# Hash attention and a gated feed-forward on one core: the second pair's hash bits, the bound's judgement, the flag read and the last additions

## The chip, the core and the metric

The kernel runs on one core of a Trainium2 chip. PE is TensorE (its weight loads, PEld, overlap its products), DVE is VectorE, ACT is ScalarE, POOL is GpSimd and SP is SyncE, which here only issues transfers. The metric is the device time in microseconds (us) of one execution. The kernel before the change has a median of 904.65 us over three runs (904.62 to 905.37).

## The reference

Two blocks follow each other. The first is attention over hash buckets: 4 batches of 8 heads, 768 positions, head dimension 64. Six sign bits of a projection give each query and key a bucket, and a key counts only for queries of its bucket. The second is a feed-forward layer with a gate of its own, over 3072 tokens, 512 wide and 2048 inside.

```python
q_bits = (np.einsum('bhsd,dk->bhsk', q, proj) > 0)      # and k_bits
mask = q_bucket[:, :, :, None] == k_bucket[:, :, None, :]
scores = np.where(mask, scale * q @ k.transpose(0, 1, 3, 2), -1e9)
attn = softmax(scores)                                  # exp(s - max) / (sum + 1e-9)
x = (attn @ v).transpose(0, 2, 1, 3).reshape(3072, 512)
h = x @ w_in
sp = np.maximum(h, 0.0) + np.log1p(np.exp(-np.abs(h)))
out = (h * erf(sp)) @ w_out
```

## The kernel before

**Attention.** Two heads form a pair, one on partitions 0 to 63 and one on 64 to 127; there are 16 pairs. A pair has four *scores* (two halves of the queries by two groups of keys), each in three chunks of 128 keys. For a chunk PE adds two products in PSUM: one over the hash bits in bf16, in which a key of another bucket gets a large negative term, and one over q and k in fp32. ACT takes the exponential, PE *weighs* the values with it, and DVE sums the exponentials over the key blocks. For the sum over partitions, the *divisor*, PE multiplies by a tile of ones. No maximum is subtracted; the kernel measures squared norms of q and k instead (`measure`, ACT) and judges later whether the bound on the scores holds (`judge`, L1743 to L1771). If it does not, the branch behind `flag` (L1776, L1777) computes everything again in a general way.

**Hash bits.** For pairs 0 and 1 they come by `hash_bits` (L377): four products with 64 output columns, into both banks of a PSUM tile. ACT takes the sign, DVE scales and doubles it in place, in `both[0]` or `both[1]`. For pairs from 2 on, `bits_of` (L845) makes four products with 32 output columns into one bank, `sign_of` (L854) and `weigh_bits` (L864) work on one [128, 384] tile, `leave_bits` (L874) writes it to DRAM and `place_bits` (L883) reads it back, as two transfers of POOL, into the rows that the scores use. The unused rows of `both[n]` must be zero; `clean` (L903) clears them on POOL after pair n's scores.

**Feed-forward.** Both products follow a scheme with seven products for eight blocks. A block p of 48 has the first products P1 to P7, which `read` (ACT) and `complete` (DVE, L1270) assemble into h, the gate (sigmoids on ACT at L1278 and L1282, multiplications on DVE at L1288), and the second products M1 to M7 (`project`, L1361). Eight blocks make a tile of 512 tokens; at its end `combine` (L1396) adds the seven banks into the output, in steps 0 to 8. The last two steps, 7 and 8, each take one half of the bank of M3. In the last tile (`t == NTILE - 1`) their results are sent from ACT's queue.

**Order.** Inside `tc.manual_schedule()` the instructions stand on each engine in the order in which they are emitted. `arrange` makes that order: a greedy planner with a cost, a rank, predecessors (`after`) and a delay to other engines (`late`) for every step. It runs once for attention and once for the feed-forward part. In attention PE's steps form one chain: the four scores of a pair, its four weighings, the bits of the pair after next and the divisor of the pair before; the bits of pair 1 stand between pair 0's scores and weighings. `start_pair` issues a pair's six transfers on SP. The weights are fetched as 32 pieces, two on SP and the rest on POOL, and converted on ACT and DVE alongside attention. The judgement is one step, `("check", 0)`, booked as 0.3 us of PE; it also carries five groups of DVE's instructions. Waits between engines are derived from the tiles that instructions read and write, in the order of emission.

Of the kernel before, what the change touches and what calls it, by code (L numbers as in the profile page):

```python
# [54 lines left out]
F32 = mybir.dt.float32  # L55
# [141 lines left out]
def kernel(  # L197
# [11 lines left out]
    nc = tc.nc  # L209
    B, H, S, D = v.shape  # L210
# [138 lines left out]

    def fetch(i, load, quick=False):  # L350
        d = dict(
            q=load.tile([P, S], F32, name="q", tag="q"),
            k=load.tile([P, S], F32, name="k", tag="k"),
            v=load.tile([P, NC, P], F32, name="v", tag="v"),
        )
        b, j = divmod(i, JP)
        parts = ((0, "q"), (0, "k"), (1, "k"), (1, "q")) if quick else ((None, "q"), (None, "k"))
        for half, what in parts:
            cols = slice(0, S) if half is None else slice(half * HS, half * HS + HS)
            queue = nc.scalar if quick and what == "k" and half == 0 else nc.sync  # L360
            for ab in range(2):
                queue.dma_start(
                    out=d[what][ab * D : ab * D + D, cols],
                    in_=qkT[2 * i + ab, "qk".index(what) * D : "qk".index(what) * D + D, cols],
                )
        for ab in range(2):
            nc.sync.dma_start(
                out=d["v"][:, :, ab * D : ab * D + D],
                in_=v[b, 2 * j + ab].rearrange("(c p) d -> p c d", p=P),
            )  # L370
        return d

# [47 lines left out]
    def attention():  # L420
        NS = NPAIR * 4
        with (
# [17 lines left out]
            e_even = ep.tile([P, NE, 2, HS + 1], F32, name="e_even")  # L440
            nc.vector.memset(e_even[:, :, :, HS : HS + 1], 1.0)
            e_odd = area[:, 0 : NE * S].rearrange("p (n a c) -> p n a c", n=NE, a=2)
            e_last = {}
# [226 lines left out]
            def divisor(i):  # L670


                d = pairs[i]
                if i == NPAIR - 1:
                    z = bank("z_ps")[:, 0:HS]
                else:
                    if i == NPAIR - 2:
                        room = pairs[i - 1]["z_room"]
                    else:
                        room = pairs[i + 3]["bits"] if i + 3 < NPAIR else big("z_ps")  # L680
                        d["z_room"] = room
                    z = room[:, 0 if i == NPAIR - 2 else 1, 0:HS]
                d["z_ps"] = z
                for half in range(2):
                    for n in range(4):
                        ab, part = divmod(n, 2)
                        nc.tensor.matmul(  # L687
                            out=z[n * QR : (n + 1) * QR, half * HS // 2 : (half + 1) * HS // 2],
                            lhsT=ones[:, 0:QR],
                            rhs=d["sum"][:, half, ab, part * HS // 2 : (part + 1) * HS // 2],  # L690
                            start=True,
                            stop=True,
                        )

# [27 lines left out]
            def spread(i):  # L722

                d = pairs[i]
                zd = d["zd"] = dram.tile([2, 4, HS // 2], F32, name="zd", tag="zd")
                d["zc"] = small.tile([P, 2 * S // P], F32, name="zc", tag="zc")
                nc.sync.dma_start(
                    out=zd.rearrange("h n c -> n h c"),
                    in_=d["z"][0 : 3 * QR + 1 : QR, 0:HS].rearrange("n (h c) -> n h c", h=2),
                )  # L730

            def gather(i):
# [3 lines left out]
                    in_=d.pop("zd")  # L736
                    .rearrange("h n c -> (h n c)")
                    .rearrange("(p c) -> p c", c=2 * S // P),
# [62 lines left out]
            def start_pair(i):  # L801
                pairs[i] = fetch(i, load)

# [30 lines left out]
            def bits_of(i):  # L834


                if i == 1:
                    hash_bits(pairs[i], big)
                    return
                d = pairs[i]  # L840
# [48 lines left out]

            def place_first():  # L890

                cols = slice(0, S)
                sign_bits(pairs[1], lambda what: both[1][:, "qk".index(what[0]), :], cols)

            def weigh_first(ab):
                spread_bits(pairs[1], slice(0, S), ab)

            def double_first():
                double_bits(pairs[1], slice(0, S))

            def clean(n):
# [6 lines left out]
            for i in range(NPAIR):  # L908
                order += [("score", 4 * i + k) for k in range(4)]
                if i == 0:  # L910
                    order.append(("bits", 1))
                order += [("weigh", 4 * i + k) for k in range(4)]
# [7 lines left out]
            for what, n in order:  # L920
                free = slots[-3] if len(slots) >= 3 else ()
                if what == "score":
                    i = n // 4
                    after = (("double_first",) if i == 1 else ("place_bits", i),)
                    for c in range(GC):
# [3 lines left out]
                elif what == "bits":  # L929
                    pe(bits_of, (n,), 0.80 if n > 1 else 1.44, (("start_pair", n),) + free)  # L930
                    slots.append((("sign_of", n),) if n > 1 else (("place_first",),))
                elif what == "divisor":
# [53 lines left out]
            for i in range(NPAIR):  # L986
                n = 4 * i
                if i:
# [3 lines left out]
                        "SP",  # L992
                        3.6,
                        (0, n - 6),
                        (("weigh", n - 9), ("bits_of", i - 1))
                        + tuple(("measure", i - 3, m, half) for m in range(2) for half in range(2)),
                        late=3.5,
                    )
                    if i == 1:
                        op(place_first, (), "ACT", 0.9, (0, n - 2, 9), (("bits_of", i),))  # L1000
                        for ab in (1, 0):
                            op(weigh_first, (ab,), "DVE", 0.43, (0, n - 2, 1), (("place_first",),))
                        op(double_first, (), "DVE", 0.35, (0, n - 2, 2), (("weigh_first", 0), ("weigh_first", 1)))
                    else:
                        op(sign_of, (i,), "ACT", 0.6, (0, n - 6, 9), (("bits_of", i), ("leave_bits", i - 1)))
                        op(weigh_bits, (i,), "DVE", 0.33, (0, n - 6, 1), (("sign_of", i),))
                        op(leave_bits, (i,), "POOL", 0.7, (0, n - 6, 2), (("weigh_bits", i),), late=4.0, far=True)
                        op(
                            place_bits,
                            (i,),  # L1010
                            "POOL",
                            1.2,
                            (0, n - 6, 3),
                            (("leave_bits", i), ("score", n - 5, 2), ("clean", i - 2)),
                            late=3.6,
                        )
                for m in range(2):
# [25 lines left out]
                op(send, (i,), "SP", 0.35, (0, n, 4), (("normalise", i),), late=2.2)  # L1043
            for n in range(2):
                op(clean, (n,), "POOL", 1.4, (0, 4 * n), (("score", 4 * n + 3, 2),), late=0.3)
            for n in range(len(pieces)):
# [154 lines left out]
    def feed_forward(check, late):  # L1201
        again = late is None
        with (
# [503 lines left out]
            if late:  # L1707
# [15 lines left out]
                for each in ops:  # L1723
                    if each.name in (("P5", 2), ("P6", 2), ("P7", 2), ("P3", 2)):
                        each.after += (("late", 6),)
                op(("check", 0), "PE", 0.3, (0, 1, 9), check, (), after=(("P3", 0), ("late", 0)), late=1.5)
                for each in ops:
                    if each.name == ("P2", FILL - 1):
                        each.after += (("check", 0),)
            else:  # L1730
                load_x(0)
                for k in range(4):
                    presum_x(0, k)
            for each in arrange(ops, dict(h=8, e=4, w=4, wt=2), PATIENCE):
                each.emit()

    flag = const.tile([1, 1], I32, name="flag")
    norms = const.tile([1, 2, 2, NPAIR], F32, name="norms")
    top = const.tile([1, 1], F32, name="top")

    def judge():

        ps = bank("bound")[:, 0 : 4 * NPAIR]  # L1743
        for ab in range(2):
# [6 lines left out]
                stop=True,  # L1751
            )
        for ab in range(2):
            nc.vector.tensor_reduce(  # L1754
# [3 lines left out]
                op=ALU.max,  # L1758
            )
        both = norms[:, :, 0, :]  # L1760
        nc.vector.tensor_tensor(out=both, in0=both, in1=norms[:, :, 1, :], op=ALU.mult)
# [9 lines left out]
        nc.vector.tensor_scalar(out=flag, in0=top, scalar1=1.0, scalar2=None, op0=ALU.add)  # L1771

    with tc.manual_schedule():
        late = attention()
        feed_forward(judge, late)
    again = nc.values_load(flag[0:1, 0:1], min_val=0, max_val=1)  # L1776
    with tc.If(again > 0):  # L1777
        general()
        feed_forward(None, None)
# [53 lines left out]
```

## Time and profile before

| what | value |
| --- | --- |
| median of three runs | 904.65 us (904.62 to 905.37) |
| the profiled execution, its own time | 904.72 us |
| its span | 902.9 us |
| granted TensorE clock, mean | 0.998 |
| PE busy | 894.3 us (99%), 5016 products |
| DVE / ACT / POOL busy | 668.5 / 563.3 / 57.9 us |
| attention, PE's first score to its last weighing | 6.1 to about 313.5 us |

A row of a group or of a timeline shows the start, the busy time, the engine, the line of the kernel, the operation, what it writes and reads, and in brackets the idle time just before it with what ended it. An engine's name with a q is its sequencer, which reads instructions ahead of the engine. "x8" is a number of instructions. A transfer's line shows the time its issue took; the time to landing is another view.

### The profile page before, as it was taken

What the parts mean: (1) busy time and instruction counts of PE and PEld (TensorE: products, weight loads), DVE (VectorE), ACT (ScalarE), POOL (GpSimd) and SP (SyncE); (2) the same over time, 40 slices, a digit from 0 to 9 for tenths busy, and PEclk for the clock granted to TensorE, in tenths of its full rate; (3) what the DMA queues carried; (4) which work ended last, traced back from release to release, by engine and by line L of the source; (5) the groups of instructions that cost most, each with busy time, mean ns of one, the idle gap of its engine ahead of it and who ended that gap; (6) DMA issues with size and microseconds to landing.
All of it is one profiled execution on the core that took longest, in us unless ns stands there. A gap on an engine that the chain in (4) does not pass through costs nothing.

```text
span 902.9 us, 12780 instructions
## 1 busy us (share of the span) xinstructions
PE 894.3 (99%) x5016; PEld 670.9 (74%) x5016; DVE 668.5 (74%) x837; ACT 563.3 (62%) x808; POOL 57.9 (6%) x95
## 2 busy tenths in 40 slices
PE   9999999999999999999999999999999999999997
PEld 5455554455544588888888888888888888888886
DVE  5999999999999879995666556666776666655652
ACT  6788888788886668855645455545655555545520
POOL 1211211111110000000000001000100010000000
PEclk9999999999999999999999999999999999999999
DMA  9547655667551322202231013211421122111211
GB/s 228 149 128 183 200 166 142 196 173 195 154 157 60 101 89 65 82 36 70 59 106 58 14 49 103 82 36 47 105 83 36 36 74 78 35 36 57 63 68 50
DMA packets 65156, 86.82 MB, mean 96 GB/s; under 512 B 34364, under 2 KB 47772, under 8 KB 65088
## 3 DMA queue, kind: packets, MB, share of 16 engines
q1 hardware_dynamic: 56528, 63.81, 24.8%
q0 software_dynamic: 8112, 21.66, 8.6%
q8 instruction: 41, 0.67, 0.3%
q10 hardware_dynamic: 448, 0.46, 0.2%
q14 instruction: 27, 0.22, 0.1%
HBM read 64.67 MB, written 17.30 MB: 91 GB/s over the span
## 4 chain that ended last, share of the span: by engine, by line
PE 99%; DVE 0%; issue 0%; ACT 0%; DVEq 0%
PE M L1361 32%; PE X L1248 29%; PE st L557 17%; PE av L642 14%; PE M L1248 3%; PE bits L845 1%; PE bits L687 1%; PE warm L807 0%; PE bits L377 0%; PE z_ps L687 0%; DVE e L1288 0%; DVE h L1270 0%; ACT both L390 0%; DVE u L1396 0%; DVE norms L1754 0%
## 5 line engine op out<-in xcount | busy, mean ns | idle before, releaser
L1288 DVE SCALAR_TENSOR_TENSOR e<-w,e 128x1024 f32<-128x1024 f32 x144 | 173.7, 1220 | 8.4 <-ACT w L1282 3.9
L1248 PE MATMUL X<-area,w_in_sb 128*128 128x256 f32 x680 | 160.6, 379 | 0.0
L1282 ACT ACTIVATE w<-h,cq 128x1024 f32<-128x1024 f32 x144 | 155.6, 1136 | 0.1
L557 PE MATMUL st<-q,k 64*128 64x384 f32 x768 | 155.1, 482 | 0.0
L1270 DVE TENSOR_TENSOR h<-X,h 128x512 f32<-128x512 f32 x65 | 44.8, 689 | 144.4 <-PE X L1248 144.4
L1248 PEld LDWEIGHTS X<-area,w_in_sb 128*128 128x128 f32 x680 | 129.2, 190 | 17.6
L1361 PE MATMUL M<-w_out_sb,h 128*128 128x256 f32 x576 | 141.1, 379 | 0.0
L1248 PE MATMUL X<-area 128*128 128x256 f32 x520 | 122.8, 379 | 0.0
L1361 PEld LDWEIGHTS M<-w_out_sb,h 128*128 128x128 f32 x576 | 109.4, 190 | 14.9
L1266 ACT COPY h<-X 128x512 f32<-128x512 f32 x85 | 49.3, 580 | 111.4 <-PE X L1248 111.3
L1248 PEld LDWEIGHTS X<-area 128*128 128x128 f32 x520 | 98.8, 190 | 13.4
L1278 ACT ACTIVATE e<-h,cq 128x1024 f32<-128x1024 f32 x48 | 55.1, 1148 | 85.9 <-DVE h L1270 85.8
L1361 PE MATMUL M<-wt,S 128*128 128x256 f32 x384 | 95.1, 379 | 0.0
L557 PEld LDWEIGHTS st<-q,k 64*128 64x128 f32 x768 | 68.8, 187 | 29.7 <-issue 27.2
L630 DVE TENSOR_TENSOR area<-area 128x1536 f32<-128x1536 f32 (+1 forms) x46 | 79.2, 1723 | 7.5 <-ACT area L584 6.3
L1361 PEld LDWEIGHTS M<-wt,S 128*128 128x128 f32 x384 | 73.0, 190 | 9.9
L584 ACT ACTIVATE e_even<-st 128x768 f32<-128x768 f32 x96 | 70.6, 822 | 0.4 <-PE st L557 0.3
L584 ACT ACTIVATE area<-st 128x768 f32<-128x768 f32 x90 | 68.0, 817 | 0.0
L642 PE MATMUL av<-e_even,v 128*64 128x385 f32 x384 | 65.6, 490 | 0.0
L557 PE MATMUL st<-both 64*128 64x384 bf16 x384 | 63.5, 323 | 0.3 <-ACT both L390 0.3
L1303 DVE TENSOR_TENSOR h<-h,e 128x1024 f32<-128x1024 f32 x48 | 57.9, 1220 | 4.6 <-ACT e L1299 4.6
L642 PE MATMUL av<-area,v 128*64 128x384 f32 x360 | 60.6, 486 | 0.0
(129 smaller groups left out, 976.8 us busy)
## 6 DMA issues: line engine op xcount, KB each, us to landing
wt<-wt SPq DMA_DIRECT2D x24, 768.0 KB, 4.2
raw<-in_w_out_dram POOLq DMA_DIRECT2D x16, 512.0 KB, 4.2
raw<-in_w_in_dram POOLq DMA_DIRECT2D x14, 512.0 KB, 4.6
v<-in_v_dram SPq DMA_DIRECT2D x32, 192.0 KB, 4.6
q<-in_qkT_dram SPq DMA_DIRECT2D x30, 192.0 KB, 4.2
k<-in_qkT_dram SPq DMA_DIRECT2D x30, 192.0 KB, 4.7
r<-rd SPq DMA_DIRECT2D x30, 192.0 KB, 3.7
xs<-x SPq DMA_DIRECT2D x15, 384.0 KB, 3.0
```

The lines of the kernel that those rows point to most:

```text
L557: nc.tensor.matmul(out=st[:, ab, 0:HS], lhsT=d["k" + src][rows, keys], rhs=d["q" + src][rows, cols], start=(part == 0), stop=(part == 1),)
L584: nc.scalar.activation(out=e[:, :, 0:HS], in_=st[:, :, 0:HS], func=AF.Exp, scale=scale)
L630: nc.vector.tensor_tensor(out=into, in0=one, in1=two, op=ALU.add)
L642: nc.tensor.matmul(out=d["av", half][rows, 0:w], lhsT=d["v"][:, g * GC + c, rows], rhs=e[:, ab, 0:w], start=(g == 0 and c == 0), stop=(g = ...
L1248: nc.tensor.matmul(out=d[where][:, u, :], lhsT=a[:, kc, f : f + P], rhs=b[:, kc, :], start=(first and u == 0 and kc == 0), stop=(last and ...
L1266: nc.scalar.copy(out=quarter(p, q), in_=st[p][where])
L1270: nc.vector.tensor_tensor(out=h, in0=st[p][where], in1=h, op=ALU.add)
L1278: nc.scalar.activation(out=s, in_=unit(p, v), func=AF.Sigmoid, bias=cq[:, n : n + 1])
L1282: nc.scalar.activation(out=q, in_=unit(p, v), func=AF.Sigmoid, scale=GATE_S[j][0], bias=cq[:, j : j + 1])
L1288: nc.vector.scalar_tensor_tensor(out=s, in0=st[p].pop(("q", v, j)), scalar=GATE_S[j][2], in1=s, op0=ALU.add, op1=ALU.mult,)
L1303: nc.vector.tensor_tensor(out=h, in0=h, in1=st[p].pop(("s", v)), op=ALU.mult)
L1361: nc.tensor.matmul(out=banks[name][:, sub, :], lhsT=a[:, u, sub * P : (sub + 1) * P], rhs=b[:, u, :], start=(c == 0 and k == 0), stop=(c = ...
```

## The change

The bits of pair 1 take the form of the later pairs. Their products stand after the second of pair 0's scores. `both[1]` is cleared by DVE at the start, and the clearing after pair 1 goes. The values of pairs 0 and 1 are fetched after the queries and keys of pair 1. A divisor is four products of 384 columns, one for each half and head, and its rows leave in that order. The judgement becomes three steps: the two products (`measured`, PE), the reductions (`judge`, DVE) and the rest (`decide`, DVE, of low rank). The flag is read (`ask`) ahead of the last tile's step 0 of `combine`. The last two products of M3 in the last block are emitted after step 7 of `combine`.

```diff
-    def fetch(i, load, quick=False):
+    def fetch(i, load, quick=False, early=False):
 ...
+        if not quick and not early:
+            fetch_v(i, d)
+        return d
+
+    def fetch_v(i, d):
+        b, j = divmod(i, JP)
 ...
+            nc.vector.memset(both[1], 0.0)
 ...
-                for half in range(2):
-                    for n in range(4):
-                        ab, part = divmod(n, 2)
-                        nc.tensor.matmul(
-                            out=z[n * QR : (n + 1) * QR, half * HS // 2 : (half + 1) * HS // 2],
-                            lhsT=ones[:, 0:QR],
-                            rhs=d["sum"][:, half, ab, part * HS // 2 : (part + 1) * HS // 2],
-                            start=True,
-                            stop=True,
-                        )
+                for n in range(4):
+                    half, ab = divmod(n, 2)
+                    nc.tensor.matmul(
+                        out=z[n * QR : (n + 1) * QR, :],
+                        lhsT=ones[:, 0:QR],
+                        rhs=d["sum"][:, half, ab, :],
+                        start=True,
+                        stop=True,
+                    )
 ...
-                zd = d["zd"] = dram.tile([2, 4, HS // 2], F32, name="zd", tag="zd")
+                zd = d["zd"] = dram.tile([4, HS], F32, name="zd", tag="zd")
                 d["zc"] = small.tile([P, 2 * S // P], F32, name="zc", tag="zc")
-                nc.sync.dma_start(
-                    out=zd.rearrange("h n c -> n h c"),
-                    in_=d["z"][0 : 3 * QR + 1 : QR, 0:HS].rearrange("n (h c) -> n h c", h=2),
-                )
+                nc.sync.dma_start(out=zd, in_=d["z"][0 : 3 * QR + 1 : QR, 0:HS])
 ...
-                pairs[i] = fetch(i, load)
+                pairs[i] = fetch(i, load, early=i == 1)
+                if i == 1:
+                    for n in range(2):
+                        fetch_v(n, pairs[n])
 ...
-                if i == 1:
-                    hash_bits(pairs[i], big)
-                    return
 ...
-            def place_first():
 ...
-            def weigh_first(ab):
 ...
-            def double_first():
 ...
-                order += [("score", 4 * i + k) for k in range(4)]
-                if i == 0:
-                    order.append(("bits", 1))
+                for k in range(4):
+                    order.append(("score", 4 * i + k))
+                    if i == 0 and k == 1:
+                        order.append(("bits", 1))
 ...
-                    after = (("double_first",) if i == 1 else ("place_bits", i),)
+                    after = (("place_bits", i),)
 ...
-                    pe(bits_of, (n,), 0.80 if n > 1 else 1.44, (("start_pair", n),) + free)
-                    slots.append((("sign_of", n),) if n > 1 else (("place_first",),))
+                    pe(bits_of, (n,), 0.80, (("start_pair", n),) + free)
+                    slots.append((("sign_of", n),))
 ...
-                        3.6,
+                        3.6 if i > 1 else 1.5,
 ...
-                        late=3.5,
 ...
+                        late=3.5 if i > 1 else 1.8,
 ...
-            for n in range(2):
-                op(clean, (n,), "POOL", 1.4, (0, 4 * n), (("score", 4 * n + 3, 2),), late=0.3)
+            op(clean, (0,), "POOL", 1.4, (0, 0), (("score", 3, 2),), late=0.3)
 ...
-                op(("check", 0), "PE", 0.3, (0, 1, 9), check, (), after=(("P3", 0), ("late", 0)), late=1.5)
+                op(("check", 0), "PE", 0.2, (0, 1, 9), check[0], (), after=(("P3", 0), ("late", 0)))
+                op(("check", 1), "DVE", 0.4, (0, 1, 9.5), check[1], (), after=(("check", 0),))
+                op(("check", 2), "DVE", 0.6, (2, 8, 0), check[2], (), after=(("check", 1),))
                 for each in ops:
                     if each.name == ("P2", FILL - 1):
-                        each.after += (("check", 0),)
+                        each.after += (("check", 1),)
             else:
                 load_x(0)
                 for k in range(4):
                     presum_x(0, k)
+            held = {("M3", NP - 1, f): None for f in (2, 3)}
             for each in arrange(ops, dict(h=8, e=4, w=4, wt=2), PATIENCE):
+                if check and each.name == ("combine", NTILE - 1, 0):
+                    check[3]()
+                if each.name in held:
+                    held[each.name] = each
+                    continue
                 each.emit()
+                if each.name == ("combine", NTILE - 1, 7):
+                    for other in held.values():
+                        other.emit()
 ...
-    def judge():
-
-        ps = bank("bound")[:, 0 : 4 * NPAIR]
+    bound = {}
+
+    def measured():
+
+        ps = bound["ps"] = bank("bound")[:, 0 : 4 * NPAIR]
 ...
+    def judge():
+
+        ps = bound["ps"]
 ...
+    def decide():
+
 ...
+    def ask():
+
+        bound["again"] = nc.values_load(flag[0:1, 0:1], min_val=0, max_val=1)
+
     with tc.manual_schedule():
         late = attention()
-        feed_forward(judge, late)
-    again = nc.values_load(flag[0:1, 0:1], min_val=0, max_val=1)
-    with tc.If(again > 0):
+        feed_forward((measured, judge, decide, ask), late)
+    with tc.If(bound["again"] > 0):
```

More of the change, by code (lines that the diff above doesn't have):

```diff
@@ L355, in fetch @@
         )
-        b, j = divmod(i, JP)
         parts = ((0, "q"), (0, "k"), (1, "k"), (1, "q")) if quick else ((None, "q"), (None, "k"))
@@ L370, in fetch @@
             )
-        return d
     def hash_bits(d, big, halves=(0, 1)):
@@ L736, in gather @@
                     in_=d.pop("zd")
-                    .rearrange("h n c -> (h n c)")
+                    .rearrange("n c -> (n c)")
                     .rearrange("(p c) -> p c", c=2 * S // P),
@@ L888, in place_bits @@
                     )
-            def place_first():
-                cols = slice(0, S)
-                sign_bits(pairs[1], lambda what: both[1][:, "qk".index(what[0]), :], cols)
-            def weigh_first(ab):
-                spread_bits(pairs[1], slice(0, S), ab)
-            def double_first():
-                double_bits(pairs[1], slice(0, S))
             def clean(n):
@@ L996, in attention @@
                         + tuple(("measure", i - 3, m, half) for m in range(2) for half in range(2)),
-                        late=3.5,
+                        late=3.5 if i > 1 else 1.8,
                     )
[L999 to L1016, printed above, removed]
+                    op(sign_of, (i,), "ACT", 0.6, (0, n - 6, 9), (("bits_of", i), ("leave_bits", i - 1)))
+                    op(weigh_bits, (i,), "DVE", 0.33, (0, n - 6, 1), (("sign_of", i),))
+                    op(leave_bits, (i,), "POOL", 0.7, (0, n - 6, 2), (("weigh_bits", i),), late=4.0, far=True)
+                    op(
+                        place_bits,
+                        (i,),
+                        "POOL",
+                        1.2,
+                        (0, n - 6, 3),
+                        (("leave_bits", i), ("score", n - 5, 2), ("clean", i - 2)),
+                        late=3.6,
+                    )
                 for m in range(2):
```

## The prediction

> **What bounds the kernel now.** I read the page first, then the waits of PE, then the timelines of the three places that the change touches: the first run, the start of the feed-forward part, the end.
>
> ```profile
> PE 894.3 (99%) x5016; PEld 670.9 (74%) x5016; DVE 668.5 (74%) x837; ACT 563.3 (62%) x808; POOL 57.9 (6%) x95
> ```
> ```profile
> PE warm L807 <- DVE ones L253: 1.0, 1, 1.0
> PE M L1248 <- DVE h L1270: 0.7, 1, 0.7
> PE st L557 <- ACT both L390: 0.3, 1, 0.3
> ```
>
> PE is busy for 894.3 of 902.9 us at full clock and waits three times, 2.0 us in all. So only four things can move the end: work taken off PE, a wait of PE removed, a new wait of PE, and the 6.66 us after PE's last product (896.20 to 902.86). Work on another engine counts only when PE waits for it.
>
> The first run, pair 1's bits and then pair 2's:
>
> ```profile
> 17.35 0.54 PE L377 MATMUL bits<-q,proj_sb 128*64 128x384 f32 x1
> 18.21 0.54 POOL L463 DMA_DIRECT2D raw<-in_w_in_dram  x1
> 18.69 4.05 PE L642 MATMUL av<-e_even,v 128*64 128x385 f32 x24
> 26.55 0.52 PE L845 MATMUL bits<-q,proj_q 128*32 128x384 f32 x2
> 27.33 0.34 PE L557 MATMUL st<-both 64*128 64x384 bf16 x2
> ```
>
> Pair 1's bits hold PE from 17.35 to 18.69, 1.34 us; pair 2's, in the other form, from 26.55 to 27.33, 0.78. Then the seam to the feed-forward part, on DVE, and what PE waited for:
>
> ```profile
> 333.96 0.45 DVE L1754 TENSOR_REDUCE norms<-bound 1x32 f32<-1x64 f32 x2 [0.88 <-PE bound L1746]
> 334.44 0.18 DVE L1761 TENSOR_TENSOR norms<-norms 1x32 f32<-1x32 f32 x1
> 335.11 2.34 DVE L1288 SCALAR_TENSOR_TENSOR e<-w,e 128x1024 f32<-128x1024 f32 x2
> 337.48 0.69 DVE L1270 TENSOR_TENSOR h<-M,h 128x512 f32<-128x512 f32 x1
> ```
> ```profile
> 338.22 3.72 PE L1248 MATMUL M<-area,w_in_sb 128*128 128x256 f32 x16 [0.66 <-DVE h L1270]
> ```
>
> The judgement holds DVE from 333.96 to 335.11, two multiplications follow, and only then comes the addition (337.48) that PE's next product into that bank needs. The planner had booked the judgement as 0.3 us of PE and nothing of DVE. Last, the end:
>
> ```profile
> 894.51 0.69 DVE L1396 TENSOR_TENSOR u<-M,u 128x512 f32<-128x512 f32 x1 [0.31 <-PE M L1361]
> 895.12 0.68 DVE L1396 TENSOR_TENSOR w<-M,w 128x512 f32<-128x512 f32 x1
> 896.24 0.76 DVE L1396 TENSOR_TENSOR u<-M,u 128x256 f32<-128x256 f32 x2 [0.44 <-PE M L1361]
> 896.69 1.84 ACTq L1405 DMA_DIRECT2D out_dram<-u  x2
> ```
> ```profile
> L1776 ACTq TENSOR_LOAD <-flag x1: 474/474/474, 898.6 to 898.6; - x1
> ```
> ```profile
> L1777 ACTq COMPARE_BRANCH  x1: 58/58/58, 899.1 to 899.1; - x1
> L1777 ACTq EVENT_SEMAPHORE  x1: 17/17/17, 901.9 to 901.9; - x1
> ```
>
> Both last additions start after the last product, though the first half was complete at 895.34. ACT sends them (0.36 and 1.44 us, to 898.53), reads the flag (to 899.05), branches at 899.12, has its next instruction at 901.88, and 0.98 us later all is over. This chain by way of ACT ends last.
>
> **The change part by part.**
>
> *Pair 1's bits on PE.* The span with its entry from the scores was 0.41 + 1.34; the new form costs 0.41 + 0.78, but stands between two score runs, so the entry to the weighing (0.41) comes on top of it and one plain step between scores (0.32) goes: 2.07 against 1.61. Gain 0.46.
>
> *Can they start earlier?* They now come after six score chunks, at about 12.4 us. Their q and k were issued from 6.08 and the last piece landed at 12.48; now pair 0's v (two transfers, 2.5 us of the same line) goes behind them, so they land near 10. That v was in at 9.1 and will be near 12; its first reader starts at 18.69. Pair 1's v keeps its place. SP issues as many transfers as before: 0.
>
> *Can they arrive in time?* On ACT the sign is shorter (0.58 for 0.90), on DVE 0.33 us stand for 1.20. New on POOL are three transfers: one out, two back. POOL loses one clearing of 1.38; DVE gets it at the start, where it waits 3.22 us for the projection with the neighbouring clearing already hoisted into the wait: 0. The sign waits behind exponentials (near 14.0), the weighting may wait behind a sum (13.82 to 15.58), so the way out starts near 16.0. In this stretch the transfer engines are over 90% busy: the weights issued at 18.21 took 7.9 us to their last landing (26.09), most pieces some 5. Pair 2's way out took 3.9. I estimate 5 to 6: back on POOL by 21 to 22, some 1.2 us to issue both, and 2.4 to 2.9 to land (pair 2's). But the planner now starts pair 1's load at 1.5 us in place of 3.6, so the first weights transfer of POOL is due 2.1 earlier and stands ahead of the way back; on the slowest engine this then ends 0.26 after the weights (so much pair 2's way out ended after those ahead of it): 26.09 + 0.26 = 26.35. PE wants the bits at 27.33 - 0.46, about 26.8. Cost 0; bounds: none, and 0.6 if an engine is a little later. Both are needed by PE alone; the weights queued behind the way back are paced for the whole attention part and can be 3 us late.
>
> *Divisors.* Eight products of 192 columns, four at a time, become four of 384. Four steps of 0.163 (the mean of one falls from 486 to 326 ns for 192 columns less) against two of 0.322: 0.65 against 0.64. Sixteen times 0.008: gain 0.13. Their transfers become simpler, 6 KB off the path: 0.
>
> *The judgement in parts.* The two products stay (0.28). The reductions (0.45) stay where they are, DVE's idle 0.88 ahead of them too; the rest (0.7) goes to a later gap of DVE (busy 74%), where its cover is DVE's slack. The multiplications start at 334.45, the addition ends near 337.5, and the product before PE's wait ends at 337.56: the 0.66 goes, and what is late next is within 0.1 us of PE itself. Product P2 of the third block, which shares the bank, now waits for the reductions, done seven us before it. Gain 0.66; bounds 0 (a new order of these steps puts another one late) and 0.7.
>
> *Flag read.* Five loads of some 0.5 us move ahead of the last additions. SP had its own at 335.2 after 3.9 us of waiting that nobody stood behind (its next transfer is at 340.45). ACT is idle 21.3 us before 885.88, DVE 2.8 us before 887.66; PE's sequencer is over 3 us ahead (its load ran at 892.17, the last product ended at 896.20). All hidden: 0, at worst 0.49 if PE had nothing queued. On ACT 0.55 us (898.57 to 899.12) leave the last chain.
>
> *First of the last additions ahead.* By the row alone the halves are apart: the second pair of products would go on under the addition, PE would still end at 896.20 and the second addition at 896.66. "PSUM — Partial Sum Buffer" of the Trainium skill, section "PSUM bank collisions raise a hardware error", speaks against it: a TensorE write and a VectorE read in one bank are to be kept apart by semaphores, whatever columns they touch, and the compiler adds a dependency there. Both halves lie in one 2 KB tile, and the row agrees: the addition waited for all four products. So issued first, it holds PE up. First addition when DVE is free (one starts 0.60 after the one before): 895.72 to 896.15. PE restarts at 896.20 and needs 0.32 + 2 x 0.216 + 0.38 = 1.13: 897.33 in place of 896.20. Second addition 897.36 to 897.78. In return the two sends lie 1.6 us apart, and I give the second 0.36 in place of 1.44 (slow ones on SP, 1.6, 1.5 and 2.2 us, also followed another send closely): 897.81 to 898.17. Branch 898.21, next instruction 2.76 later at 900.97, end at 901.95 in place of 902.86: gain 0.91. SP comes near: the last landing, 2.2 after 897.81, is 900.0, and SP's row of waits took 0.97 after it. I take 0.86; bounds a loss of 0.2 (the second send still takes 1.44) and a gain of 2.0, which is what the row alone would allow at most (sends at 896.18 and 896.69, landing 898.9, end 900.85). By the rule the sum is 902.6, by the row 902.5 to 901.5.
>
> *Sum.* 0.46 + 0.13 + 0.66 + 0.86 = 2.11. The profiled execution took 904.72: 902.61. It stands 0.07 above the median of 904.65; so 902.6.
>
> **The rivals.** A measurement of this kernel tells about 0.2% (1.8 us) from no change: faster is below 902.84, slower above 906.46.
>
> 1. *The end gives nothing* (the held products cost what the load and the second send return, or a late landing keeps SP): 902.6 + 0.9 = 903.5. For it: PE's tail grows by 1.13 and nothing here shows a lone send by ACT. Against: slow sends were close followers. Chance 0.13.
> 2. *The seam's wait moves*: the feed-forward order is planned anew, and a wait of 0.5 to 0.7 stays: 903.2. For it: DVE is near full at 345 to 370. Against: the cost is now booked where it falls. Chance 0.11.
> 3. *Slower: pair 1's bits come too late for its first score.* Two trips stand in the most crowded stretch. If each took the 7.9 us of the weights: 16.0 + 7.9 + 1.2 + 7.9 = 33.0, PE idle 6.2, 908.7; at 31, 4.2 us, 906.8. It decides from a landing at 28.9 (loss 2.1) and is slower by over 0.2% from 30.7. Against: 96 and 42 KB, not 512. Chance 0.16, at 906.8.
> 4. *The halves run side by side after all*, or the last landing comes early: 901.7. Chance 0.10.
>
> **How the numbers follow.** The sum as worked out has 0.50, at 902.6 with 0.3 to either side; 0.08 of it lies within 0.2%. Faster: 0.42 + 0.10 = 0.52. Same: 0.08 + 0.13 + 0.11 + 0.01 = 0.33. Slower: 0.15. The range goes from rival 4 (901.7) past rivals 1 and 2 with a stall of up to 0.6 each: 904.3; what lies above is most of rival 3.
>
> **What would show it.** Right: 32-column bits for pair 1 near 12.4; the last transfer into both below 26.8 and no wait of PE at its first score; no wait of PE near 338; the first last addition near 895.7, a wait of PE for it of some 0.8 us, the second send at 0.36 us, no flag load between it and the branch, and 4.6 us from PE's last product to the end. Wrong: a new wait of PE above 0.5 us anywhere, above all near 26.8; the last products going on under the addition; a second send of 1.4 us.

## The result and the profile after

The changed kernel takes 903.0 us (median of 19 runs, 902.67 to 904.01); the kernel before took 904.79 us in the same sessions (19 runs, 903.58 to 905.56). The ratio is 0.9984, 95% interval 0.9977 to 0.9991: 1.45 us faster, between 0.8 and 2.1. The profiled execution took 902.87 us. The forecast was 902.6, range 901.7 to 904.3.

First the page's engine line, then PE's waits. PE runs 128 products fewer, eight for each of the 16 divisors. (Its busy time is no measure of the gain: the same kernel has 893.8 us here and 894.4 in w1.) The wait near 338 is gone, and a new one of 0.8 us on an addition of the output has come:

```profile
PE 893.8 (99%) x4888; PEld 665.9 (74%) x4888; DVE 667.5 (74%) x836; ACT 563.7 (63%) x808; POOL 58.1 (6%) x97
```
```profile
PE warm L811 <- DVE ones L253: 1.0, 1, 1.0
PE M L1345 <- DVE u L1380: 0.8, 1, 0.8
PE st L562 <- ACT both L394: 0.3, 1, 0.3
```

The timeline of the first run: pair 1's bits stand at 12.32 with 32 columns, and pair 1's first score follows pair 2's bits at once, without a wait:

```profile
12.32 0.52 PE L846 MATMUL bits<-q,proj_q 128*32 128x384 f32 x2
18.05 1.19 PE L647 MATMUL av<-e_even,v 128*64 128x385 f32 x6
25.95 0.52 PE L846 MATMUL bits<-q,proj_q 128*32 128x384 f32 x2
26.74 0.34 PE L562 MATMUL st<-both 64*128 64x384 bf16 x2
```

POOL's timeline of that stretch: the way out at 16.03, the clearing, a piece of the weights, 3.81 us of waiting for the way out, and the way back at 23.21:

```profile
16.03 0.55 POOL L875 DMA_DIRECT2D bd<-sg  x1 [13.46 <-DVE sg L865]
17.54 1.38 POOL L893 MEMSET both<- 128x1536 bf16 x1 [0.96 <-PE st L562]
18.86 0.54 POOL L468 DMA_DIRECT2D raw<-in_w_in_dram  x1
23.21 1.14 POOL L884 DMA_DIRECT2D both<-bd  x2 [3.81 <-DMA bd<-sg]
```

DVE at the seam: only the reductions are left there, and the addition at 336.05 now ends at 336.74. PE's next product into that bank starts at 336.80, 0.27 us after the product before it in place of the usual 0.22: the addition is still late, by 0.05 us.

```profile
333.30 0.45 DVE L1755 TENSOR_REDUCE norms<-bound 1x32 f32<-1x64 f32 x2 [0.88 <-PE bound L1743]
333.68 2.34 DVE L1272 SCALAR_TENSOR_TENSOR e<-w,e 128x1024 f32<-128x1024 f32 x2
336.05 0.69 DVE L1254 TENSOR_TENSOR h<-M,h 128x512 f32<-128x512 f32 x1
...
392.73 0.17 DVE L1765 TENSOR_TENSOR norms<-norms 1x32 f32<-1x32 f32 x1
```

The end. The first half's addition starts at 894.29 in place of waiting for the last product, PE stands until it is over, and the two sends are 1.6 us apart (0.36 and 0.34 us):

```profile
893.69 0.68 DVE L1380 TENSOR_TENSOR w<-M,w 128x512 f32<-128x512 f32 x1
894.29 0.41 DVE L1380 TENSOR_TENSOR u<-M,u 128x256 f32<-128x256 f32 x1
894.40 0.37 SPq L1389 DMA_DIRECT2D out_dram<-w  x1
894.74 1.99 ACTq L1389 DMA_DIRECT2D out_dram<-u  x2
894.76 0.73 PEld L1345 LDWEIGHTS M<-w_out_sb,S 128*128 128x128 f32 x4 [1.25 <-DVE u L1380]
894.76 1.13 PE L1345 MATMUL M<-w_out_sb,S 128*128 128x256 f32 x4 [0.85 <-DVE u L1380]
895.93 0.42 DVE L1380 TENSOR_TENSOR u<-M,u 128x256 f32<-128x256 f32 x1 [1.23 <-PE M L1345]
```
```profile
L1784 ACTq COMPARE_BRANCH  x1: 58/58/58, 896.8 to 896.8; - x1
L1784 ACTq EVENT_SEMAPHORE  x1: 17/17/17, 899.6 to 899.6; - x1
```

**Where the time came from.** The start of an execution, up to PE's first product over pair 0's bits, took 8.2 to 9.2 us in twelve profiles and follows no edit that I can see (one kernel had 8.21 in one profile and 8.85 in another: after and w1). From there on the stretches repeat within some 0.1 us, with two exceptions: the end, which scatters by 0.26 in the five profiles with the products held and the flag read early, u3 and v3 apart (4.95 to 5.21), and the stretch of attention in v2, v3 and w2, which is 0.24 to 0.34 longer because pair 1's bits came late there (see v3). So the stretches, and not spans or medians, carry the small verdicts below. Each column is the time from the mark before it, in us, read from the starts of PE's rows:

| kernel | to pair 1's first score | to the feed-forward part | to the bound's products | to PE's last product | to the end | sum |
| --- | --- | --- | --- | --- | --- | --- |
| before | 18.93 | 286.13 | 20.18 | 562.56 | 6.66 | 894.46 |
| after | 18.53 | 286.07 | 20.17 | 562.91 | 5.19 | 892.88 |
| u1 without held products | 18.53 | 286.07 | 20.17 | 561.79 | 5.76 | 892.33 |
| u2 flag read late | 18.53 | 286.07 | 20.17 | 562.91 | 5.03 | 892.71 |
| u3 judgement at once | 18.53 | 286.08 | 20.17 | 563.68 | 7.19 | 895.65 |
| u4 old bits | 18.93 | 286.04 | 20.17 | 562.91 | 5.07 | 893.12 |
| v1 as u3, one ACT instruction more | 18.53 | 286.08 | 20.17 | 563.68 | 5.21 | 893.67 |
| v2 bits after four scores | 19.63 | 286.31 | 20.17 | 562.91 | 4.95 | 893.97 |
| v3 no branch | 18.53 | 286.41 | 20.17 | 562.90 | 3.31 | 891.33 |
| v4 one last addition | 18.53 | 286.09 | 20.17 | 561.79 | 5.39 | 891.97 |
| w1 after again | 18.53 | 286.08 | 20.17 | 562.91 | 5.01 | 892.70 |
| w2 v4, weights behind the bits | 18.53 | 286.31 | 20.17 | 561.80 | 5.66 | 892.47 |

After against before: 0.40 in the first run, 0.06 in attention, and then PE's last product 0.35 later but the end 1.47 sooner behind it. Sum 1.58; the profiled spans differ by 1.77 because the start happened to be 0.19 shorter.

### The profile page after: what moved, and what is told of

It reads as the page before. It is cut to its first block, busy times and chain, and to the rows that moved or that the text cites. A ratio compares the mean times of both kernels' runs of the same rounds, so it can differ in the third digit from the quotient of the medians.

```text
span 901.1 us, 12520 instructions
## 1 busy us (share of the span) xinstructions
PE 893.8 (99%) x4888; PEld 665.9 (74%) x4888; DVE 667.5 (74%) x836; ACT 563.7 (63%) x808; POOL 58.1 (6%) x97
## 4 chain that ended last, share of the span: by engine, by line
PE 99%; DVE 0%; issue 0%; ACT 0%
PE M L1345 32%; PE X L1232 29%; PE st L562 17%; PE av L647 14%; PE M L1232 4%; PE bits L846 1%; PE bits L691 1%; PE warm L811 0%; PE z_ps L691 0%; PE bits L381 0%; DVE u L1380 0%; ACT both L394 0%; PE bound L1743 0%; DVE ones L253 0%; DVE w L1380 0%
```

## The experiments

**u1: the products not held.**

```diff
-            held = {("M3", NP - 1, f): None for f in (2, 3)}
+            held = {}
```

> The changed kernel, but the last two products of M3 in their old place (before step 7 of combine); all else stays. Theory A (the prediction's: the products wait for the addition in their bank, 1.0 us of PE, and this is paid back by a second send of 0.34 us): no wait of PE at the end, PE ends some 1.0 us earlier than in the changed kernel, near 894.9; the two sends are 0.4 us apart again and the second takes about 1.4 us, so the end comes at 900.9 to 901.1, the same as changed (within 0.2 us). Theory B (holding the products costs more than it returns): the second send is short without it, the end comes near 900.4, 0.6 us faster than the changed kernel. Theory C (holding returns more than it costs): the end comes later than 901.3.

Measured: 902.77 us, ratio to before 0.9983 (0.9974 to 0.9992). PE no longer waits at the end and is 1.12 us earlier (561.79 against 562.91); the sends are close again:

```profile
894.53 0.68 DVE L1380 TENSOR_TENSOR w<-M,w 128x512 f32<-128x512 f32 x1
895.24 0.37 SPq L1389 DMA_DIRECT2D out_dram<-w  x1
895.65 0.76 DVE L1380 TENSOR_TENSOR u<-M,u 128x256 f32<-128x256 f32 x2 [0.44 <-PE M L1345]
896.11 1.57 ACTq L1389 DMA_DIRECT2D out_dram<-u  x2
```

The second send took 1.17, not the 1.44 of theory A and not the short one of theory B. The end moved back by only 0.57 to 0.75 (5.76 against 5.19 and 5.01), so the profile is 0.37 to 0.55 us better without holding, more than the end's scatter. B's verdict holds, by another way than it said; the medians (902.77 against 903.0 to 903.19) agree but are too near each other to show it alone.

**u2: the flag read after everything.**

```diff
-                if check and each.name == ("combine", NTILE - 1, 0):
-                    check[3]()
...
         feed_forward((measured, judge, decide, ask), late)
+    ask()
```

> The changed kernel, but the flag is read after everything, as before the change. Theory A (ACT's chain of send, flag load, branch and next instruction ends last, as in the profile before): the end is 0.55 us later, span near 901.6. Theory B (in the changed kernel the landing of the last send and SP's row of waits after it end last: ACT's instruction after the branch stands at 899.63, SP comes to it at 900.12, so ACT has 0.5 us of slack): the load fills that slack, the end is 0 to 0.1 us later, span near 901.1 to 901.2, and the early flag read is worth almost nothing beside the held products.

Measured: 903.04 us, ratio 0.9984 (0.9975 to 0.9993); the end is 5.03 us after PE's last product, level with the changed kernel's 5.01 and 5.19. Theory B: beside the held products the early flag read is worth nothing. With u1 the parts of the end can be set side by side. I take PE's column and the end's together, and for neither part the kernel before less the judgement's 0.77 (u3): neither 568.45, flag alone 567.55, holding alone 567.94, both 567.92 to 568.10. Alone they are worth 0.90 and 0.51, together 0.35 to 0.53. (No run had neither of them in the changed kernel, so the first figure is worked out and not measured; each of the others is one profile or two.) They cut the same piece of ACT's chain: before, SP waited 0.7 us for ACT at the end, so that ACT's chain ended last; in u2 it waits 0.2, and in the changed kernel there is no such wait. Before, then u2:

```profile
SPq L1829 <- ACTq L1777: 0.7, 1, 0.7
```
```profile
SPq L1835 <- ACTq L1783: 0.2, 1, 0.2
```

**u3: the judgement in one step, and v1: the same with one instruction more.** In u3 one step calls `measured`, `judge` and `decide`, booked as 0.3 us of PE, as before the change. v1 adds a copy of 128 x 1 on ACT, which is idle there.

```diff
-                op(("check", 0), "PE", 0.2, (0, 1, 9), check[0], (), after=(("P3", 0), ("late", 0)))
-                op(("check", 1), "DVE", 0.4, (0, 1, 9.5), check[1], (), after=(("check", 0),))
-                op(("check", 2), "DVE", 0.6, (2, 8, 0), check[2], (), after=(("check", 1),))
+                op(("check", 0), "PE", 0.3, (0, 1, 9), at_once, (), after=(("P3", 0), ("late", 0)), late=1.5)
...
-                        each.after += (("check", 1),)
+                        each.after += (("check", 0),)
```

```diff
+        pad = const.tile([P, 1], F32, name="pad")
+        nc.scalar.copy(out=pad, in_=sgn)
         bound["again"] = nc.values_load(flag[0:1, 0:1], min_val=0, max_val=1)
```

> The changed kernel, but the judgement is one step again, booked as 0.3 us of PE, with all five groups of DVE's instructions in it. Theory A (DVE's late addition held PE): a wait of PE of 0.6 to 0.7 us for the addition at L1254 some 5 us after the bound's products, and the span 0.65 us longer. Theory B (the wait went because of the new order from the first run, not because of the split): no wait there, span as the changed kernel's 901.1.

> The kernel with the judgement in one step (u3), and one tiny copy more on ACT, 128 x 1, beside the flag read, where ACT is idle: no work of the kernel changes. In u3 the end took 7.2 us after PE's last product in place of 5.1, since ACT stood 2.6 us between its first and its second instruction after the branch, with a fetch of instructions in between; u3 has one ACT instruction fewer than the changed kernel. Theory A (where the branch's target falls in a fetched piece[...] sets this): with one instruction more the second fetch goes, the end is back at 5.0 to 5.2 us after PE, while the wait of 0.66 us near 338 stays: 2.0 to 2.2 us faster than u3, 0.7 us slower than the changed kernel. Theory B (the late end belongs to the judgement's order): the end stays at 7.2 us.

Measured: u3 906.21 us, ratio 1.0018 (1.0009 to 1.0027), slower even than before; v1 903.83 us, ratio 0.9996 (0.9987 to 1.0005). In u3 the wait is back as theory A says, and PE's column is 0.77 longer:

```profile
335.41 2.34 DVE L1272 SCALAR_TENSOR_TENSOR e<-w,e 128x1024 f32<-128x1024 f32 x2
337.77 0.69 DVE L1254 TENSOR_TENSOR h<-M,h 128x512 f32<-128x512 f32 x1
```
```profile
PE M L1232 <- DVE h L1254: 0.7, 1, 0.7
```

The other 2 us of u3 are not the judgement's. ACT's sequencer in u3, the branch, its first instruction after it and the next one (the kernel's last line, L1838), and then the same in v1:

```profile
L1786 ACTq COMPARE_BRANCH  x1: 58/58/58, 898.5 to 898.5; - x1
L1786 ACTq EVENT_SEMAPHORE  x1: 17/17/17, 901.2 to 901.2; - x1
```
```profile
L1838 ACTq DRAIN  x2: 8/72/135, 903.8 to 904.2; - x2
```
```profile
L1788 ACTq COMPARE_BRANCH  x1: 58/58/58, 897.6 to 897.6; - x1
L1788 ACTq EVENT_SEMAPHORE  x1: 17/17/17, 900.5 to 900.5; - x1
```
```profile
L1840 ACTq DRAIN  x2: 8/8/8, 900.5 to 901.3; - x2
```

From 901.2 to 903.8 ACT has nothing to do and gets no instruction. One instruction more, which does no work of the kernel, and the gap is gone: the end is 5.21 in place of 7.19 us, the median 2.4 us lower. So the late end does not belong to the judgement's order, and what theory A of v1 forecast came. In u3 the trace has a fetch of instructions (8 KB) from 901.85 to 902.4, begun 0.6 us after ACT's first instruction and ahead of the late one. That ACT waited for it is read from the order alone, and it accounts for half a microsecond of the 2.6; v1 shows that one instruction decides, not why. The trace counts 982 instructions of ACT in the changed kernel and in v1, 981 in u3: the changed kernel stands one instruction from this edge.

**u4: pair 1's bits as before.** The hunks of `fetch`, `start_pair`, `bits_of`, the order of PE and the clearing are undone; two of them are shown.

```diff
-                for k in range(4):
-                    order.append(("score", 4 * i + k))
-                    if i == 0 and k == 1:
-                        order.append(("bits", 1))
+                order += [("score", 4 * i + k) for k in range(4)]
+                if i == 0:
+                    order.append(("bits", 1))
...
+                if i == 1:
+                    hash_bits(pairs[i], big)
+                    return
```

> The changed kernel, but pair 1's bits, its transfers and the place of the first values as before the change. Theory A: PE needs 0.4 to 0.46 us more from its first bits product to pair 1's first score (22.0 us in place of 21.6), the rest is as in the changed kernel, the span is 0.4 us longer. Theory B (the way through DRAM costs PE waits in some executions, which the one profile of the changed kernel missed by 0.1 us: the last piece landed at 26.65 and PE's score starts at 26.74): the times of this kernel scatter less than the changed kernel's, and its median is level with it or faster.

Measured: 903.53 us, ratio 0.999 (0.9981 to 0.9999). Theory A: the first stretch is 18.93 again, 0.40 longer, the rest as changed. The median is 0.3 to 0.5 us above the changed kernel's (903.19 in w1, 903.0), and the times (903.2 to 904.14) scatter as much as those of w1 (0.94 against 0.98 us from lowest to highest). So theory B's forecast fails, though the wait that it feared does occur, in v3.

**v2: the bits later.**

```diff
-                    if i == 0 and k == 1:
+                    if i == 0 and k == 3:
```

> The changed kernel, but pair 1's bits after all four scores of pair 0, some 4.8 us later, and still by way of DRAM. Theory A (the trip of 13.5 us from the bits to the landing has no slack left, as 26.65 against 26.74 says): the trip starts 4.8 us later, in transfer engines that empty meanwhile, lands at 27.5 to 31, and PE waits at pair 1's first score for 1 to 4 us; the kernel is slower than changed by as much, near 904 to 907. Theory B (the trip's end is set by the queue ahead of it, the weights that land by 24.1, and not by its start): it lands before 27.0 and PE waits under 0.3 us.

Measured: 905.05 us (904.48 to 908.93), ratio 1.0015 (1.0006 to 1.0024): slower than before. The way out starts 5.6 us later than in the changed kernel, but takes 3.1 in place of 6.9 us, and the way back ends near 28.5 in place of 26.7 (0.5 of it is this execution's later start):

```profile
21.59 0.55 POOL L875 DMA_DIRECT2D bd<-sg  x1 [2.50 <-DVE sg L865]
25.01 1.20 POOL L884 DMA_DIRECT2D both<-bd  x2 [2.88 <-DMA bd<-sg]
```
```profile
PE st L562 <- DMA both<-bd: 1.1, 1, 1.1
```

So both theories are half right: the trip gives back most of a late start, but the slack was small, and what is left is PE's wait, one for one. The first stretch is 1.10 longer by the first of the two transfers back; the second one, landed at 28.55, holds the next product and makes attention 0.24 longer.

Why the trip gives time back is in the transfers of the changed kernel. The way out was issued at 16.03, but from 16 to 20 us only the queue of SP's transfers (q1) moved anything, one fetch of instructions apart. POOL's queue (q0) has its first packet at 20.5. The rows show packets, MB and the share of the 16 engines' time, from 16 to 20 us and then from 20 to 24:

```profile
q1 hardware_dynamic: 1174, 0.93, 109.6%
```
```profile
q0 software_dynamic: 192, 0.62, 42.2%
q1 hardware_dynamic: 727, 0.29, 37.4%
```

In the kernel before, the weights issued at 18.21 had their first packet at 20.5 too, and in v2, with no way out ahead of them, at 20.3. So an earlier issue gained nothing here. Whether SP's transfers held it up or something else did is open. The slower executions of v2, up to 908.93, fit longer waits; no profile of one of them shows it.

**v3: no branch.** The flag read, the branch and the general way behind it are left out; the judgement is computed.

> The changed kernel without the flag read, the branch and the general way behind it; the judgement is still computed. Theory A (the end is set by the landing of the last send, which the fetches of instructions behind the branch disturb, and by SP's row of waits): without fetches the last landing is 1.7 us after the send's start in place of 2.8, the end 4.0 to 4.3 us after PE's last product in place of 5.2, about 1 us faster than the changed kernel. Theory B (the landing alone): 0 to 0.2 us faster.

Measured: 901.4 us (9 runs), ratio 0.9968 (0.9958 to 0.9978). The end comes 3.31 us after PE's last product, 1.7 to 1.9 us sooner, nearly twice what theory A gave. The last send lands 1.7 us after its start in place of 2.8, as theory A said, and SP then needs 0.27 us in place of 1.04: three of its waits stand behind the landing, where the changed kernel has fifteen. The flag read is worth nothing beside the held products (u2), so the branch is what costs, more than anything that this change moved.

This profile shows one thing more, about the bits. The second transfer back landed at 27.69, after PE's first score of pair 1 had begun, and the second product of that score, which waits for it, starts at 27.73 and not beside the first at 27.39. The two products, 0.34 us in the changed kernel, take 0.68:

```profile
27.39 0.68 PE L562 MATMUL st<-both 64*128 64x384 bf16 x2
```

Nothing in v3's edit lies near this place. In the eight profiles that have the trip as the changed kernel has it, the last landing lies from 0.94 us ahead of the score (u1) to 0.30 behind it (v3).

**v4: one last addition, one send.** Without holding; steps 7 and 8 become one of 128 x 512; four tiny copies on ACT keep clear of the edge of u3. Two hunks of it:

```diff
-                subs = slice(*subs)
+                subs = slice(0, 2) if k == 7 and t == NTILE - 1 else slice(*subs)
...
+                        if k == 8 and t == NTILE - 1:
+                            continue
```

> The changed kernel without the held products, and with the last two additions as one (128 x 512, 0.69 us) and their two sends as one on ACT; four tiny copies on ACT keep its instruction count clear of the edge seen in u3. Theory A (holding costs PE 1.0 us and returns 0.6; a second send close behind the first costs 0.8 us in u1): one send of 0.39 us starts 0.75 us after PE's last product and nothing follows it, the end is 5.4 to 5.6 us after PE's last product, against 5.77 in u1 and 5.17 + 1.1 in the changed kernel: some 0.7 us faster than the changed kernel, near 902.3. Theory B (the larger send lands later): as u1, 902.8.

Measured: 902.88 us (902.1 to 904.23), ratio 0.9982 (0.9973 to 0.9991).

```profile
895.65 0.69 DVE L1380 TENSOR_TENSOR u<-M,u 128x512 f32<-128x512 f32 x1 [0.44 <-PE M L1345]
896.37 0.40 ACTq L1389 DMA_DIRECT2D out_dram<-u  x1
```

The profile is as theory A has it (5.39 against 5.76 in u1; the sum 0.7 to 0.9 us under the changed kernel's). But w2, with the same end, has 5.66, so that the gain over u1 is 0.1 to 0.4 and no more than the end scatters. The median is as theory B has it, 902.88, and the runs cannot tell v4 from u1.

**w1 and w2: the changed kernel again, and v4 with the third piece of the weights behind the way back of pair 1's bits.**

```diff
-                    (("start_pair", 1), ("fetch_weights", n - 1), ("add_rest", n - 3), ("exponential", max(PACE * n // 10 - 2, 0), 1)),
+                    ((("place_bits", 1),) if n == 2 else ()) + (("start_pair", 1), ("fetch_weights", n - 1), ("add_rest", n - 3), ("exponential", max(PACE * n // 10 - 2, 0), 1)),
```

> The changed kernel once more, beside w2 on the same chip. From PE's first full score to the end its profile took 892.9 us, and the start before it took 8.2 us in that execution but up to 9.2 in others, whatever the kernel: median 902.8 to 903.4.

> v4 (no held products, one last addition and one send, four tiny copies on ACT) with the third piece of the weights behind the way back of pair 1's bits on POOL. Theory A (what the segments of the profiles show adds up): from the first full score to the end 892.0 us as in v4, 0.9 less than the changed kernel, and the bits land some 2 us ahead of PE's score instead of 0.1 to 0.7; the median is 0.7 to 0.9 us under w1. Theory B (the gain is smaller than what the start scatters): level with w1 within 0.4 us.

Measured: w1 903.19 us (902.85 to 903.83), w2 902.88 us (901.89 to 904.14), ratios to before 0.9982 (0.9973 to 0.9991) and 0.9979 (0.9970 to 0.9988). Level: theory B. The bits do not land sooner in w2; the last landing, at 27.73, is 0.15 us behind the score's start and holds PE for 0.2. POOL's timeline of w2:

```profile
16.88 0.55 POOL L875 DMA_DIRECT2D bd<-sg  x1 [14.31 <-DVE sg L865]
18.39 1.38 POOL L893 MEMSET both<- 128x1536 bf16 x1 [0.96 <-PE st L562]
23.55 1.18 POOL L884 DMA_DIRECT2D both<-bd  x2 [3.79 <-DMA bd<-sg]
24.72 0.58 POOL L468 DMA_DIRECT2D raw<-in_w_in_dram  x1
```

The way back waits for the way out until 23.55 all the same and then needs 3.1 to 3.6 us; this piece of the weights was not what it stood behind. No version tried here is shown to beat the changed kernel by its times.

## Why the prediction was right, point by point

- **Pair 1's bits: 0.46 forecast, 0.40 measured** (u4). The step was right: up to the first weighing PE is 0.45 sooner, and 0.05 is lost from there to pair 1's first score.
- **The trip: in time in seven of eight profiles, and in part by luck.** I had the way out at 16.0 (16.03), an estimate of 5 to 6 us for it (6.9 here, 5.5 to 6.6 in the seven other profiles of the same trip), the way back at 2.4 to 2.9 (2.9 to 3.1) and the landing at 26.35 for a need at 26.8. The second transfer back, issued at 23.78, landed 2.9 us later, some 0.1 us ahead of the score at 26.74. The result held, but the reason that I gave for the landing, the weights ahead of it, was wrong (w2): the way out itself was the long piece, and for its first 4.5 us nothing of it moved. In v3 the same trip came 0.30 late and cost 0.34. So rival 3's mechanism is real, at a few tenths; v2 shows its price of one for one. The microseconds that it feared did not come.
- **Divisors: 0.13 forecast, 0.06 measured** over the 15 divisors of the attention stretch (0.09 in u4, which has the new divisors and the old bits). The direction was right, the size under what these profiles can settle.
- **The judgement: 0.66 forecast, 0.77 measured** (u3 and v1). The cost, the place and the next lateness (within 0.1 us of PE; the addition is 0.05 late now) were right. The row's 0.66 is short because it counts from the end of the product before, 0.38 us after that one's start, while products start 0.22 apart: from start to start the trace has 1.04 us at this place before the change and 0.27 after it, 0.77 less.
- **The held products: PE later by 1.13 forecast, 1.12 measured** (u1). The last products waited for the addition in their bank (0.85 us in the row above), as I took from the rule of "PSUM — Partial Sum Buffer", and both sends came out short, 0.36 and 0.34. Both halves also lie in one tile, so this does not show whether the tile or the bank asked for the wait.
- **The end: this is the step that was mis-sized.** I summed ACT's chain, from the send to the branch to its next instruction, as if it ended last, and took 0.86 for flag read and held products together; the runs give 0.35 to 0.53. After the change ACT's instruction stands at 899.6; the last landing comes at 899.15 and SP's row of waits behind it ends at 900.15, so that the end, 5.19 us after PE, comes by way of SP. I had the landing 2.2 us after the send's start, from other sends, where it took 2.8, and 0.05 us of difference between the two chains; the end behind PE was 0.6 us longer than the 4.6 that I worked out. So the 0.55 us of the flag load were counted along a chain that had become the shorter one (u2), and the held products cost more than they brought (u1).
- **The sum: 2.11 forecast, 1.58 in the profile's stretches,** 1.45 by the ratio. The missing 0.5 is the end's. Rival 1 (the end gives nothing, 903.5) came half true. Rivals 2 and 4 did not come. By the line that I drew for "faster", 902.84, the median of 903.0 falls just on the side of "same", to which I had given 0.33 against 0.52; the interval of the ratio lies clear of no change all the same.

## What to carry to other kernels

Where the last engine has two chains behind it, cut both or neither: two edits that shorten the same chain do not add, and the second shows nothing once the other chain ends last. A step that costs nothing on an engine in the planner's books may still hold the busiest engine through the order it makes; book it where it runs. And an unchanged part may turn slower by a change of the instruction count: look at the gap after a branch before blaming the edit. Before pricing a transfer by its size, look at which queues move anything in the stretch where it is issued.

## What the runs showed of the hardware

A taken branch was expensive and uneven. ACT had its next instruction 2.5 to 3.0 us after the branch's start in these profiles (2.76 in the one before, u3's second gap apart), and the kernel without it ended 1.7 to 1.9 us sooner (v3). "Runtime: NRT & Kernel Launch" of the Trainium skill, section "Instruction fetch mechanics", says that a taken branch to a page that is not held forces a fetch. The traces agree as far as they go: in the changed kernel's, three pieces of 8 KB are fetched between ACT's branch at 896.75 and its next instruction at 899.62, and in v3's none is fetched in the last 6 us. What I had not expected is a second gap of 2.6 us behind the branch, and that a single tiny instruction on ACT took it away (u3 and v1). That the place where the branch's target falls decides this is my inference.

Transfers of POOL moved nothing while those of SP filled the transfer engines: issued at 16.03 in the changed kernel and at 18.21 in the one before, they have their first packet at 20.5 in both. The cause is open.

A second send of ACT within 0.4 us of the first took 1.44 and 1.17 us, one 1.6 us after the first 0.34; one send of twice the size took 0.40.
